# Weights' words joined by two VectorE operations out of PSUM, squares of two quads on TensorE, smaller first MLP groups, a new order

## The chip, the core and the metric

The kernel runs on one core of a Trainium2 chip. Its engines are TensorE (PE in the profile), VectorE (DVE), ScalarE (ACT), GpSimd (POOL) and SyncE (SP), which here issues nearly all DMAs from one queue, in order. The metric is the device time of one launch in microseconds; lower is better.

## What is computed

```python
scores = scale * np.matmul(q, k.transpose(0, 1, 3, 2))          # 4 batches, 8 heads, 576 x 576, head size 64
thresh = np.max(scores, axis=-1, keepdims=True) - tau
scores = np.where(scores >= thresh, scores, -1000000000.0)
attn = softmax(scores); x = np.matmul(attn, v)                  # heads side by side: x is (4, 576, 512)
...
xn = (x - mu) / np.sqrt(var + 1e-06) * g_ln
x = x + np.maximum(xn @ w_ch1, 0.0) @ w_ch2                     # 512 -> 2048 -> 512
...
theta = x @ w_theta
y = w_tok_r @ (x * cos(theta)) + w_tok_i @ (x * sin(theta))     # mixes the 576 tokens
u = x + y; out = u + np.maximum(u @ w_ch, 0.0)
```

Everything is f32 outside. Inside, a matmul of f32 accuracy is three fp16 matmuls: each operand is scaled by a power of two and split into a high and a low fp16 part.

## The kernel before

**Three kinds of work.** (1) Attention: 36 units of 128 query rows for each of the 4 batches, 144 in all; two heads are done together as a "couple" of two units (one unit for the half tile at a batch's end). A unit is a QK product on PE (tile `S`), the row minimum on VectorE (`top`), a mask and an exp on ScalarE, a high fp16 part (`hi16`) and a low one (`lo16`) on whichever of VectorE, GpSimd, ScalarE the plan picks, a transposing DMA of the result (`PT`), and the product with V on PE (`pv`). (2) The MLP on the finished tokens: nine tiles of 128 tokens for batches 0 and 1 ("the first half"), nine for batches 2 and 3. Tiles go in groups of three; for each group a layer norm, a transpose on PE (`ptr`, split into `xt`), and 16 chunks, each a first product (`p`, 12 matmuls whose moving operand is the group's 384 tokens) and a second one (`ch`, 3 matmuls of 512 columns per tile). (3) The token mixing (`th`, `y`, `o`) from about 640 us on.

**Weights.** w1 and w2 come as 32 pieces of 128 x 512 in four "quads" of eight; `th`, `tok` and `cw` are 20 more. Their two 32-bit halves arrive as pairs of integers (`raw`) and are joined into f32 words on the chip (class `Piece`): `s1` scales the high half (GpSimd or ScalarE), `s1b` the low half (ScalarE), `s2b` and `s2c` shift and put in the sign (VectorE), `s3` adds the low half (GpSimd). `sq` squares the words on ScalarE to find the scale (`pow2` sums over partitions and rounds to a power of two), and `split` makes the two fp16 parts. A quad of `HOME` (0 and 1) has its raw words loaded into the 16 weight buffers themselves; the others go through a ring of three raw buffers.

**The order is planned by the program itself.** `Plan.run` is a list scheduler: each operation has costs for the engines that may do it, due-time offsets by kind (`OFF`), extra costs of an engine (`PEN`) and buffers that it takes and gives back (`Slot`, `Res`). The instructions are written out on each engine in the order that this plan finds; on the chip each engine runs them strictly in that order and waits by semaphores. Where the plan sees PE idle for over 200 ns before `turn`, `keep` writes warming matmuls (`warm`) into the gap. Four PSUM banks (`rM`) serve `p`, `ch`, `pv`, `ptr` and the small sums; two more pairs serve `S`.

Of the kernel before, what the change touches and what calls it, by code (L numbers as in the profile page):

```python
# [21 lines left out]
DM = 512  # L22
KB = 4
# [37 lines left out]
HPA = 0.0  # L61
# [6 lines left out]
MX = 1  # L68
# [140 lines left out]
def tile_kernel(  # L209
# [39 lines left out]
    def vc(n, x=1.04):  # L249
        return 157.0 + x * n  # L250
# [54 lines left out]
    def n_tile(slot, name):  # L305
        return lp.tile([128, 512], F32, tag=str(slot), name=name)
# [57 lines left out]

    warm = Slot(rM)
# [20 lines left out]
    class Piece:  # L386


        def __init__(self, src, shape, ss, col, name, start, kind, home=False, by=None):
# [12 lines left out]

            def s1(e):
                st["a"] = n_tile(sa, f"a_{name}")[:, 0:n]
                if e is G:
                    G.tensor_scalar(out=st["a"], in0=st["rw"][:, :, 1].bitcast(F32), scalar1=DOWN, scalar2=0.0,  # L406
                                    op0=ALU.mult, op1=ALU.add)
                else:
                    A.activation(out=st["a"], in_=st["rw"][:, :, 1].bitcast(F32), func=AF.Copy, scale=DOWN)

            def s1b(e):
                rw = st["rw"]
                A.activation(out=rw[:, :, 0], in_=rw[:, :, 0].bitcast(U32), func=AF.Copy, scale=2.0 ** -29)
# [22 lines left out]
            o = op(s2b, [o], V=vc(n, .95), **kw)
            o = op(s2c, [o], (), [sa], V=vc(n, 1.45), **kw)
            self.done = last_s3[0] = op(s3, [o, ob, last_s3[0]], () if home else (self.sf,), () if home else (sl,), G=gadd(n), **kw)
            self.sq = op(sq, [self.done] + ([] if by is None else [k_load]), A=ac(n) + 130.0, **kw)

        def split(self, hi, lo, sc, deps, acq=()):
# [17 lines left out]
            return op(s5, [o], (), [self.sf], V=vc(n, 1.4), G=2000, **kw)  # L459

    def pow2(nm, ss, n, top, deps, dst, kind):
# [24 lines left out]
        o = op(add_up, [o], (), (ms,), V=170, **kw)  # L486
# [16 lines left out]
    class Quad:  # L503


        def __init__(self, q, prev):
# [312 lines left out]
    def unit(st, us, o_qk, pen0, kw, cp):  # L819
# [136 lines left out]
    def ln_group(p, gi, base):  # L956
# [85 lines left out]
        for r0, r1 in zip(ROUNDS, ROUNDS[1:]):  # L1042
            qd = quads[r0 // 4]
            for t in range(nt):
                ms = Slot(rM)
                o = None
                for i in range(r0, r1):
# [10 lines left out]
                    o = op(mm, [o or hs[r1 - 1][3], hs[i][2], chunks[i].c2], (ms,) if i == r0 else (), rel, T=3 * mm_(512),  # L1058
# [88 lines left out]
    def split_weight(name, src_list, start, sc, kind="cvt"):  # L1147
# [523 lines left out]
```

## Time and profile before

| | |
|---|---|
| median of 3 runs | 890.38 us (890.22 to 890.48) |
| profiled execution, its own time | 890.8 us |
| its span, first to last instruction | 889.0 us |
| mean granted TensorE clock | 0.984 of full speed |
| busy: PE, DVE, ACT, POOL | 836.2, 670.4, 575.8, 503.4 us |
| PE's part in it that is `warm` filling | 70.1 us |

Busy time is the union of an engine's instructions. PE looks busy for 94% of the span, but 70 us of this are matmuls whose result nobody reads. The shares change much between the stages, so the stages are read apart.

### The profile page before, as it was taken

How to read it: one execution, taken by the hardware profiler on the slowest of the kernel's cores; microseconds unless marked ns; L12 is line 12 of the kernel's file. 1: busy time of each engine (PE TensorE's matmuls, PEld its weight loads, DVE VectorE, ACT ScalarE, POOL GpSimd, SP SyncE). 2: the span in 40 equal slices, each digit the busy share in tenths (PEclk: the TensorE clock that was granted, in tenths of full speed). 3: DMA queues.
4: the chain of work that ended last, by engine and by line, in shares of the span. 5: the costliest groups of instructions: out<-in, count | busy, mean ns of one | idle time of the engine just before them, and what ended most of it. 6: DMA issues, size and time to landing. Idle time of an engine off the chain costs nothing.

```text
span 889.0 us, 19045 instructions
## 1 busy us (share of the span) xinstructions
PE 836.2 (94%) x7368; PEld 563.5 (63%) x7368; DVE 670.4 (75%) x1250; ACT 575.8 (65%) x1075; POOL 503.4 (57%) x554
## 2 busy tenths in 40 slices
PE   9687777999999999999999999999999799989997
PEld 8575566656666666675666556555556477666776
DVE  5999999979898874795278725666688974699943
ACT  6787887777898875895388724555567542465512
POOL 5999999887657851692067403343437570064910
PEclk9899999999999999999999999999999899999999
DMA  8955888846799744891566428234213011020011
GB/s 278 255 127 138 161 189 166 210 93 93 136 187 201 140 94 94 162 173 31 127 115 109 81 57 196 64 119 150 75 36 107 25 36 54 1 77 1 1 55 54
DMA packets 209211, 99.36 MB, mean 112 GB/s; under 512 B 173280, under 2 KB 193760, under 8 KB 209120
## 3 DMA queue, kind: packets, MB, share of 16 engines
q1 hardware_dynamic: 208832, 98.14, 49.1%
q8 instruction: 58, 0.95, 0.5%
q14 instruction: 33, 0.27, 0.1%
q10 hardware_dynamic: 288, 0.00, 0.0%
HBM read 46.21 MB, written 9.44 MB: 63 GB/s over the span
## 4 chain that ended last, share of the span: by engine, by line
PE 68%; DVE 15%; POOL 10%; issue 5%; DMA 1%; ACT 1%; DVEq 0%; POOLq 0%; SPq 0%
PE ch L598 20%; PE p L575 20%; PE S L770 6%; PE y L1491 6%; PE pv L792 6%; PE o L1549 3%; PE th L1315 2%; POOL ringP L241 2%; POOL ringP L238 2%; DVE z L1380 1%; DVE raw_w L422 1%; POOL a_w L406 1%; POOL f_w L426 1%; DVE ringE L830 1%; PE warm L371 1%
## 5 line engine op out<-in xcount | busy, mean ns | idle before, releaser
L598 PE MATMUL ch<-w,h 128*128 128x512 f16 x864 | 199.8, 379 | 0.3 <-DVE x L1063 0.3
L575 PE MATMUL p<-xt,w 128*128 128x384 f16 x1152 | 198.2, 326 | 0.0
L241 POOL TENSOR_TENSOR ringP<-ringE,ringP 128x512 f16<-128x512 f32 (+2 forms) x146 | 144.2, 1001 | 54.2 <-DVE h L584 29.1
L575 PEld LDWEIGHTS <-w 128*128 128x128 f16 x1152 | 110.0, 98 | 73.2 <-issue 2.8
L598 PEld LDWEIGHTS <-h 128*128 128x128 f16 x864 | 81.5, 98 | 90.0 <-issue 3.5
L830 DVE TENSOR_SCALAR_CACHE_REDUCE ringE<-S 128x576 f32<-128x576 f32 x144 | 104.6, 748 | 15.7 <-PE S L770 13.2
L770 PE MATMUL S<-khi,q 64*128 64x288 f32 (+1 forms) x576 | 85.2, 328 | 28.6 <-DVE ringE L830 25.2
L846 ACT ACTIVATE ringE<-ringE,thr 128x576 f32<-128x576 f32 x144 | 105.6, 767 | 7.5 <-POOL thr L838 5.5
L876 ACT ACTIVATE ringE<-ringE,ntaup 128x576 f32<-128x576 f32 x144 | 104.2, 764 | 0.1
L1491 PE MATMUL y<-tok,z 128*128 128x288 f16 x768 | 99.6, 289 | 0.0
L1063 DVE SCALAR_TENSOR_TENSOR x<-ch,inv,x 128x512 f32<-128x512 f32 x72 | 53.7, 747 | 58.0 <-PE ch L598 57.8
L238 POOL TENSOR_SCALAR ringP<-ringE 128x576 f16<-128x576 f32 x93 | 68.6, 744 | 49.3 <-ACT ringE L876 48.2
L581 ACT ACTIVATE h<-p 128x384 f16<-128x384 f32 x96 | 46.8, 488 | 71.0 <-PE p L575 70.4
L1491 PEld LDWEIGHTS <-z 128*128 128x128 f16 x768 | 76.1, 99 | 21.0
L584 DVE SCALAR_TENSOR_TENSOR h<-p,h 128x384 f16<-128x384 f32 x96 | 52.5, 550 | 45.7 <-ACT h L581 45.0
L792 PEld LDWEIGHTS <-PT 128*128 128x128 f16 (+1 forms) x2240 | 77.1, 101 | 14.6 <-issue 5.6
L770 PEld LDWEIGHTS S<-khi,q 64*128 64x128 f32 (+1 forms) x576 | 55.6, 191 | 48.5 <-DVE ringE L830 31.1
L792 PE MATMUL pv<-va,PT 128*128 128x65 f16 (+1 forms) x2240 | 81.2, 194 | 1.4 <-DMA PT<-ringP 0.9
L241 DVE TENSOR_TENSOR ringP<-ringE,ringP 128x512 f16<-128x512 f32 (+1 forms) x78 | 70.6, 918 | 3.9 <-POOL ringP L238 3.0
L379 PE MATMUL warm<-one 128*128 128x256 bf16 x538 | 70.1, 286 | 0.0
L379 PEld LDWEIGHTS <-one 128*128 128x128 bf16 x538 | 53.4, 104 | 10.6 <-issue 2.8
L1549 PE MATMUL o<-x1T,cw 128*128 128x288 f16 x384 | 48.2, 286 | 2.5 <-POOL x1T L241 2.5
(246 smaller groups left out, 1398.4 us busy)
## 6 DMA issues: line engine op xcount, KB each, us to landing
raw_w<-in_w SPq DMA_DIRECT2D x32, 512.0 KB, 4.7
raw_tok<-in_wtok SPq DMA_DIRECT2D x12, 432.0 KB, 3.3
qraw<-in_qT SPq DMA_DIRECT2D x20, 256.0 KB, 3.4
vraw<-in_v SPq DMA_DIRECT2D x16, 320.0 KB, 4.7
kraw<-in_kT SPq DMA_DIRECT2D x16, 288.0 KB, 4.0
xfin<-x SPq DMA_DIRECT2D x18, 256.0 KB, 2.0
xl<-xfin SPq DMA_DIRECT2D x18, 256.0 KB, 3.3
out<-uo SPq DMA_DIRECT2D x16, 288.0 KB, 2.1
```

Source lines behind the costliest of these rows:

```text
L238: G.tensor_scalar(out=out, in0=in_, scalar1=1.0, scalar2=0.0, op0=ALU.mult, op1=ALU.add)
L241: e.tensor_tensor(out=out, in0=a, in1=b, op=ALU.subtract)
L379: T.matmul(w[:, 0:256], lhsT=one16[:, 0:128], rhs=one16, start=True, stop=True)
L575: T.matmul(st["ps"][:, :n], lhsT=ch.w1(a, c), rhs=xt()[:, c, bb, :n], start=(kk == 0), stop=(kk == 11))
L598: T.matmul(ps, lhsT=h[:, a, t * 128:(t + 1) * 128], rhs=ch.w2(bb), start=(first and (a, bb) == M2[0]), stop=(stop and (a, bb) == M2[2]))
L770: T.matmul(w["S"][:, n, 0:288], lhsT=qd.q["t"][r, a, hp], rhs=d.k[bb][r, n * 288:(n + 1) * 288], start=(k == 0), stop=(k == 2))
L792: T.matmul(out[:, j * 65:j * 65 + n], lhsT=l, rhs=r[:, j * 65:j * 65 + n], start=(k == 0), stop=(k == len(seq) - 1))
L830: V.tensor_scalar(out=st["e"].rearrange("p (a k) -> p a k", a=2), in0=st["S"][:, :, 0:288], scalar1=-1.0, scalar2=None, op0=ALU.mult, op1= ...
L846: A.activation(out=st["e"], in_=st["e"], func=AF.Prelu, bias=cp["thr"][:, j:j + 1], scale=-1.0, alpha=STEEP)
L876: A.activation(out=e_of(ws), in_=e_of(ws), func=AF.Exp, bias=ntaup, scale=1.0)
L1491: T.matmul(st["ps"][n][:, 0:288], lhsT=a, rhs=w[:, n * 288:(n + 1) * 288], start=(k == 0 and q == 0), stop=(k == 8 and q == 2))
L1549: T.matmul(st["ps"][n][:, 0:288], lhsT=w[:, cs], rhs=d["t"][a][:, kk, n * 288:(n + 1) * 288], start=(kk == 0 and q == 0), stop=(kk == 3 an ...
```

## The change

The joining of words loses `s2b`, `s2c` and GpSimd's add. ScalarE alone now scales the high half, and writes it to one of the four `rM` banks of PSUM (tile `a`); VectorE then takes the sign from it into the low half (`s2`) and shifts it by three bits over the low half (`s3`), both times reading `a` out of PSUM. For quads 0 and 1 the squares come from PE: each 128 x 128 block of a piece, its words' upper halves read as bf16, is multiplied by itself into one bank (`gram`), and VectorE reads the largest entry. No quad is at home any more: all pieces load into the ring of three raw buffers. The first half's MLP groups hold two, two, two and three tiles in place of three times three. The exp of a couple's two units is one instruction (`MX = 2`). The constants that set the order are new.

```diff
-CVQ = (8000.0, 30000.0, 30000.0, 30000.0)
-CVD = 2300.0
-HOME = (0, 1)
-GROUPS = (((0, 3), (3, 3), (6, 3)), ((0, 3), (3, 3), (6, 3)))
+CVQ = (8000, 36900, 69900, 8000)
+CVD = 3600.0
+HOME = ()
+SQ = 'TTAA'
+SQP = 'A'
+GROUPS = (((0, 2), (2, 2), (4, 2), (6, 3)), ((0, 3), (3, 3), (6, 3)))
...
-HPA = 0.0
+HPA = 1500.0
...
-MX = 1
+MX = 2
...
-            sa = Slot(rN)
+            sa = Slot(rM)
...
             def s1(e):
-                st["a"] = n_tile(sa, f"a_{name}")[:, 0:n]
-                if e is G:
-                    G.tensor_scalar(out=st["a"], in0=st["rw"][:, :, 1].bitcast(F32), scalar1=DOWN, scalar2=0.0,
-                                    op0=ALU.mult, op1=ALU.add)
-                else:
-                    A.activation(out=st["a"], in_=st["rw"][:, :, 1].bitcast(F32), func=AF.Copy, scale=DOWN)
+                st["a"] = m_tile(sa, [128, 512], f"a_{name}")[:, 0:n]
+                A.activation(out=st["a"], in_=st["rw"][:, :, 1].bitcast(F32), func=AF.Copy, scale=DOWN)
...
-            def s2b(e):
-                a = st["a"].bitcast(U32)
-                V.tensor_scalar(out=st["rw"][:, :, 1].bitcast(U32), in0=a, scalar1=3, scalar2=0x7FFFFFF8,
-                                op0=ALU.logical_shift_left, op1=ALU.bitwise_and)
-
-            def s2c(e):
-                a, y = st["a"].bitcast(U32), st["rw"][:, :, 1].bitcast(U32)
-                V.scalar_tensor_tensor(out=y, in0=a, scalar=0x80000000, in1=y, op0=ALU.bitwise_and, op1=ALU.bitwise_or)
+            def s2(e):
+                low = st["rw"][:, :, 0].bitcast(U32)
+                V.scalar_tensor_tensor(out=low, in0=st["a"].bitcast(U32), scalar=0x80000000, in1=low, op0=ALU.bitwise_and,
+                                       op1=ALU.bitwise_or)
 
             def s3(e):
...
-                G.tensor_tensor(out=st["w"].bitcast(I32), in0=st["rw"][:, :, 1], in1=st["rw"][:, :, 0], op=ALU.add)
+                V.scalar_tensor_tensor(out=st["w"].bitcast(U32), in0=st["a"].bitcast(U32), scalar=3,
+                                       in1=st["rw"][:, :, 0].bitcast(U32), op0=ALU.logical_shift_left, op1=ALU.bitwise_or)
...
+                    for k in range(0, n, 128):
+                        T.matmul(stats.ps[:, 0:128], lhsT=w[:, k:k + 128], rhs=w[:, k:k + 128], start=(col == 0 and k == 0),
+                                 stop=(col == 3 and k + 128 == n))
```

The order shows where this moves the work. First place: VectorE, where the first MLP group's operand `xt_0_0` is finished; `ringE,bt_b_t_h` is the row minimum of the couple of batch b, tile t, heads h. Before:

```order
L830 TENSOR_SCALAR ringE_83,bt_1_4_0_0_2309<-S_1_4_0_0_2280 128x576
L241 TENSOR_TENSOR xt_0_0_2265<-ptr_0_0_1_2273,xt_0_0_2265 128x4x128
L241 TENSOR_TENSOR xt_0_0_2265<-ptr_0_0_2_2299,xt_0_0_2265 128x4x128
L241 TENSOR_TENSOR ringP_84<-ringE_83,ringP_84 128x512
L417 TENSOR_SCALAR raw_w1_12_3_2185<-a_w1_12_3_2332 128x512
```

And with the change:

```order
L920 TENSOR_SCALAR ringE_83,bt_0_3_1_0_1510<-S_0_3_1_1_1449 128x576
L243 TENSOR_TENSOR xt_0_0_1528<-ptr_0_0_0_1512,xt_0_0_1528 128x4x128
L563 TENSOR_SCALAR sc_1_114<-t2_w2_1_119 128x1
L567 TENSOR_SCALAR sc_1_114<-sc_1_114 128x1
L446 SCALAR_TENSOR_TENSOR raw_w1_8_2_1415<-a_w1_8_2_1561,raw_w1_8_2_1415 128x512
L243 TENSOR_TENSOR xt_0_0_1528<-ptr_0_0_1_1521,xt_0_0_1528 128x4x128
```

The operand was finished behind the minimum of couple 1_4_0 (the 21st), with the pieces of quad 3 (`w1_12`) already under way; now it is finished behind couple 0_3_1 (the 14th), with quad 2 (`w1_8`) at its third piece. Second place: VectorE in quad 1, the joining of words. Before:

```order
L417 TENSOR_SCALAR raw_w1_4_2_644<-a_w1_4_2_762 128x512
L417 TENSOR_SCALAR raw_w1_4_3_710<-a_w1_4_3_786 128x512
L684 SCALAR_TENSOR_TENSOR va_0_3_548<-vraw_0_3_313,vscale0_91,va_0_3_548 128x10x64
L422 SCALAR_TENSOR_TENSOR raw_w1_4_2_644<-a_w1_4_2_762,raw_w1_4_2_644 128x512
L830 TENSOR_SCALAR ringE_83,bt_0_1_1_0_935<-S_0_1_1_0_873 128x576
L830 TENSOR_SCALAR ringE_83,bt_0_1_1_0_935<-S_0_1_1_1_874 128x576
L422 SCALAR_TENSOR_TENSOR raw_w1_4_3_710<-a_w1_4_3_786,raw_w1_4_3_710 128x512
```

And with the change:

```order
L446 SCALAR_TENSOR_TENSOR raw_w1_4_2_810<-a_w1_4_2_915,raw_w1_4_2_810 128x512
L446 SCALAR_TENSOR_TENSOR raw_w1_4_3_895<-a_w1_4_3_966,raw_w1_4_3_895 128x512
L451 SCALAR_TENSOR_TENSOR f_w1_4_2_996<-a_w1_4_2_915,raw_w1_4_2_810 128x512
L920 TENSOR_SCALAR ringE_83,bt_0_2_0_0_1002<-S_0_2_0_0_977 128x576
L451 SCALAR_TENSOR_TENSOR f_w1_4_3_1018<-a_w1_4_3_966,raw_w1_4_3_895 128x512
```

There are still two VectorE operations for a piece, but `a` now lies in PSUM and the second one gives the finished word `f`, so GpSimd's add behind it is gone. Third place: SP's queue, the same quad. Before:

```order
L898 DMA_TRANSPOSE PT_0_0_1_1_551<-ringP_84 128x9x128
L401 DMA raw_w1_4_0_596<-in_w1 128x1024
L401 DMA raw_w1_4_1_632<-in_w1 128x1024
L401 DMA raw_w1_4_2_644<-in_w1 128x1024
L401 DMA raw_w1_4_3_710<-in_w1 128x1024
L401 DMA raw_w2_4_0_756<-in_w2 128x1024
L401 DMA raw_w2_4_1_768<-in_w2 128x1024
L898 DMA_TRANSPOSE PT_0_0_2_0_782<-ringP_84 128x9x128
```

And with the change:

```order
L434 DMA raw_w1_4_0_704<-in_w1 128x1024
L434 DMA raw_w1_4_1_718<-in_w1 128x1024
L990 DMA_TRANSPOSE PT_0_0_3_0_759<-ringP_84 128x9x128
L990 DMA_TRANSPOSE PT_0_0_3_1_773<-ringP_84 128x9x128
L434 DMA raw_w1_4_2_810<-in_w1 128x1024
L990 DMA_TRANSPOSE PT_0_1_0_0_820<-ringP_84 128x9x128
L990 DMA_TRANSPOSE PT_0_1_0_1_868<-ringP_84 128x9x128
L434 DMA raw_w1_4_3_895<-in_w1 128x1024
```

The loads of quad 1 stood in a row, each into a buffer of its own; now they stand one or two at a time between the transposes, each waiting for one of three raw buffers.

## Rows read from the trace of the kernel before

**Rows 1.** Busy time by stage; columns: length, PE, PEld, DVE, ACT, POOL, clock, DMA.

```profile
0.00:157.00 157.00, 122.14 (x1287) 101.91 (x1288) 142.59 (x254) 124.34 (x231) 142.13 (x159) 0.93 0.78 188
157.00:296.00 139.00, 138.16 (x1440) 88.50 (x1437) 121.81 (x252) 113.95 (x221) 100.36 (x122) 1.00 0.79 154
296.00:640.00 344.00, 343.81 (x3003) 210.42 (x3001) 219.15 (x457) 219.31 (x427) 155.53 (x196) 1.00 0.52 112
640.00:889.00 249.00, 232.13 (x1645) 162.65 (x1643) 186.84 (x290) 118.22 (x199) 105.37 (x80) 0.98 0.12 40
```

**Rows 2.** The same view, the warming matmuls of L379 alone (PE, PEld).

```profile
0.00:157.00 157.00, 70.11 (x538) 53.40 (x538) 0.93 0.78 188
```

**Rows 3.** Tile p, first 200 us: shortest, median, longest; first and last start.

```profile
L575 PE MATMUL p<-xt,w x96: 322/326/337, 156.9 to 188.1; 128*128 128x384 f16 x96
```

**Rows 4.** Who waited for whom, 0 to 157: total us, times, longest.

```profile
PE S L770 <- DVE ringE L830: 25.0, 22, 3.6
```

**Rows 5.** Groups by shape, 0 to 157: busy us, mean ns, idle before.

```profile
L422 DVE SCALAR_TENSOR_TENSOR raw_w<-a_w,raw_w 128x512 uint32<-128x512 uint32 x27 | 32.3, 1201 | 0.0
L830 DVE TENSOR_SCALAR_CACHE_REDUCE ringE<-S 128x576 f32<-128x576 f32 x37 | 26.8, 746 | 2.5 <-PE S L770 2.1 <-POOL ringP L241 0.4
L241 POOL TENSOR_TENSOR ringP<-ringE,ringP 128x512 f16<-128x512 f32 x18 | 26.0, 1446 | 0.0
L238 POOL TENSOR_SCALAR ringP<-ringE 128x576 f16<-128x576 f32 x30 | 25.2, 849 | 0.7 <-ACT ringE L876 0.7
L426 POOL TENSOR_TENSOR raw_w<-raw_w 128x512 int32<-128x512 int32 x16 | 20.1, 1258 | 0.7 <-DVE raw_w L422 0.7
L417 DVE TENSOR_SCALAR raw_w<-a_w 128x512 uint32<-128x512 uint32 x27 | 19.4, 730 | 1.2 <-POOL a_w L406 1.2
L241 DVE TENSOR_TENSOR ringP<-ringE,ringP 128x512 f16<-128x512 f32 x16 | 18.5, 1163 | 1.3 <-POOL ringP L238 1.3
L452 DVE SCALAR_TENSOR_TENSOR w<-raw_w,sc,w 128x512 f16<-128x512 f32 x13 | 16.1, 1279 | 0.0
L406 POOL TENSOR_SCALAR a_w<-raw_w 128x512 f32<-128x512 f32 x17 | 14.4, 845 | 0.6 <-DVE raw_w L422 0.6
L426 POOL TENSOR_TENSOR f_w<-raw_w 128x512 int32<-128x512 int32 x10 | 12.8, 1280 | 0.0
L409 ACT ACTIVATE a_w<-raw_w 128x512 f32<-128x512 f32 x11 | 7.3, 665 | 2.5 <-DVE raw_w L422 2.5
```

**Rows 6.** Groups by shape, 157 to 296.

```profile
L241 POOL TENSOR_TENSOR ringP<-ringE,ringP 128x512 f16<-128x512 f32 x20 | 23.8, 1192 | 0.8 <-ACT ringP L234 0.4
L238 POOL TENSOR_SCALAR ringP<-ringE 128x576 f16<-128x576 f32 x33 | 23.1, 707 | 21.0 <-ACT ringE L876 21.0
L1063 DVE SCALAR_TENSOR_TENSOR x<-ch,inv,x 128x512 f32<-128x512 f32 x16 | 11.8, 744 | 3.6 <-PE ch L598 3.4
```

**Rows 7.** PE in order of time at 296 us.

```profile
296.42 0.53 PE L770 MATMUL S<-khi,q 64*128 64x288 f32 x4
```

**Rows 8.** Busy time by stage of L770 (S), then L575 (p), L598 (ch), L792 (pv).

```profile
0.00:156.90 156.90, 31.83 (x228) 23.39 (x228) 0.93 0.78 188
156.90:296.40 139.50, 23.47 (x252) 18.18 (x252) 1.00 0.79 154
...
156.90:296.40 139.50, 50.31 (x288) 26.94 (x288) 1.00 0.79 154
...
156.90:296.40 139.50, 46.73 (x198) 18.32 (x198) 1.00 0.79 154
...
156.90:296.40 139.50, 24.96 (x679) 23.02 (x675) 1.00 0.79 154
```

**Rows 9.** The page's group of matmuls with 288 columns.

```profile
L1491 PE MATMUL y<-tok,z 128*128 128x288 f16 x768 | 99.6, 289 | 0.0
```

**Rows 10.** SP's own waits, 0 to 157.

```profile
SPq L401 <- POOL f_w L426: 7.4, 6, 2.3
```

More of the change, by code (lines that the diff above doesn't have):

```diff
@@ L363, in tile_kernel, with g_square, g_turn, g_top @@
     k_pool = op(c_pool, [k_ones], G=1200, kind="prep")
+    gg = const.tile([128, KB], F32, name="gg")
+    gmax = const.tile([128, 1], F32, name="gmax")
+    gtop = const.tile([128, 1], F32, name="gtop")
+    gt, sg = {}, Slot(rM)
+    def g_square(e):
+        V.tensor_tensor(out=gg, in0=gsb, in1=gsb, op=ALU.mult)
+    def g_turn(e):
+        gt["ps"] = psM.tile([128, 512], F32, tag=str(sg), name="gtop_ps")
+        T.matmul(gt["ps"][0:KB, 0:128], lhsT=gg, rhs=ident, start=True, stop=True)
+    def g_top(e):
+        V.tensor_scalar(out=gt["ps"][0:KB, 0:128], in0=gt["ps"][0:KB, 0:128], scalar1=1.0, scalar2=None, op0=ALU.mult, op1=ALU.max,
+                        accum_out=gmax[0:KB])
+    def g_sum(e):
+        T.matmul(gt["ps"][:, 256:257], lhsT=ones[0:KB], rhs=gmax[0:KB], start=True, stop=True)
+    def g_keep(e):
+        V.tensor_copy(out=gtop, in_=gt["ps"][:, 256:257])
+    o = op(g_square, [k_load], V=120, kind="prep")
+    o = op(g_turn, [o, k_pool], (sg,), T=230, key=-1e6, kind="prep")
+    o = op(g_top, [o], V=300, kind="prep")
+    o = op(g_sum, [o, k_ones], T=60, key=-1e6, kind="prep")
+    k_top = op(g_keep, [o], (), (sg,), V=160, kind="prep")
     warm = Slot(rM)
@@ L432, in __init__ @@
             kw = dict(kind=kind)
             self.load = op(s0, start, (sl,), Q=1800, **kw)
-            o = op(s1, [self.load], [sa], A=ac(n) + 40.0, G=gs(n), **kw)
             ob = op(s1b, [self.load], A=ac(n), **kw)
[L436 to L439, printed above, removed]
+            o = op(s1, [self.load], [sa], A=ac(n) + 40.0, **kw)
@@ L441, in split @@
+            o = op(s2, [o, ob], V=vc(n, 1.15), **kw)
+            self.done = last_s3[0] = op(s3, [o, last_s3[0]], () if home else (self.sf,), (sa,) if home else (sa, sl), V=vc(n, 1.15), **kw)
+            if how == "T":
+                self.sq = op(sq, [self.done] + stats.deps, () if col else (stats.sl,), T=n / 128.0 * mm_(128), key=-9e5, **kw)
+                stats.deps = [self.sq]
+            else:
+                self.sq = op(sq, [self.done], **cost(how, n), **kw)
         def split(self, hi, lo, sc, deps, acq=()):
@@ L458, in split, with measure, __init__, __call__ @@
             o = self.hi_op = op(s4, [self.done, self.sq] + deps, acq, A=ac(n) + 93.0, V=vc(n, .95), **kw)
[L459 to L461 removed]
+            return op(s5, [o], (), [self.sf], V=vc(n, 1.4), G=gr(n), **kw)
+    def measure(out, in_, acc):
+        A.activation(out=out, in_=in_, func=AF.Square, accum_out=acc)
+    class Stats:
+        def __init__(self, nm):
+            self.nm, self.t = nm, None
+            self.sl, self.ps, self.deps = Slot(rM), None, []
+        def __call__(self):
+            if self.t is None:
+                self.t = sm.tile([128, 4, 6], F32, tag="st4", bufs=4, name="st_" + self.nm)
+            return self.t
+    def cost(how, n):
+        return {"A": ac(n) + 130.0} if how == "A" else {"V": vc(n)}
+    def squares_of(how, ss, n, stats_, deps, kind, by=None):
+        if how == "A" and by is None:
+            return deps
+        def go(e):
+            if how == "T":
+                V.tensor_scalar(out=stats_.ps[:, 0:128], in0=stats_.ps[:, 0:128], scalar1=1.0, scalar2=None, op0=ALU.mult, op1=ALU.max,
+                                accum_out=ss[:, 0:1])
+                return
+            if how == "V":
+                stats = stats_()
+                V.tensor_tensor(out=stats[:, :, 0:5:4], in0=stats[:, :, 1:5:3], in1=stats[:, :, 1:5:3], op=ALU.mult)
+                V.scalar_tensor_tensor(out=stats[:, :, 2:6:3], in0=stats[:, :, 0:5:4], scalar=n / 2.0,
+                                       in1=stats[:, :, 2:6:3], op0=ALU.mult, op1=ALU.add)
+                V.tensor_tensor(out=ss, in0=stats[:, :, 2], in1=stats[:, :, 5], op=ALU.add)
+            if by is not None:
+                V.tensor_tensor(out=ss, in0=ss, in1=by, op=ALU.mult)
+                V.tensor_tensor(out=ss, in0=ss, in1=by, op=ALU.mult)
+        if how == "T":
+            return [op(go, deps, (), (stats_.sl,), V=360, kind=kind)]
+        return [op(go, deps, V=(420 if how == "V" else 0) + (0 if by is None else 280), kind=kind)]
+    def pow2(nm, ss, n, top, deps, dst, kind, by=None):
         st, ms = {}, Slot(rM)
@@ L536, in parts @@
                 return ends
-            rm1 = const.tile([128, KB], F32, name=f"rm1_{q}")
-            p1 = pieces("w1", [w1[c * 128:(c + 1) * 128, fc * 256:fc * 256 + 1024] for c in range(KB)], rm1, True)
-            o1 = pow2(f"w1_{q}", rm1, KB, W1_TOP, [pc.sq for pc in p1], sc[:, 0:1], kd)
+            gram = SQ[q] == "T"
+            nr = 1 if gram else KB
+            rm1 = const.tile([128, nr], F32, name=f"rm1_{q}")
+            p1, st1 = pieces("w1", [w1[c * 128:(c + 1) * 128, fc * 256:fc * 256 + 1024] for c in range(KB)], rm1)
+            o1 = squares_of(SQ[q], rm1, DM, st1, [k_load] + [pc.sq for pc in p1], kd, None if gram else gsb)
+            o1 = pow2(f"w1_{q}", rm1, nr, W1_TOP, o1, sc[:, 0:1], kd, gtop if gram else None)
             def gscale(e):
@@ L891, in go @@
             def go(e):
-                sub(e, p_of(ws)[:, :, 576:640], e_of(ws)[:, :, 512:576], p_of(ws)[:, :, 512:576])
+                crossed = len(ws) == 2 and (ws[0]["es"].i < ws[1]["es"].i) != (ws[0]["s16"].i < ws[1]["s16"].i)
+                for w_ in ([[w] for w in ws] if crossed else [ws]):
+                    sub(e, p_of(w_)[:, :, 576:640], e_of(w_)[:, :, 512:576], p_of(w_)[:, :, 512:576])
             return go
```

55 lines of the change are left out of this document (35 added, 20 removed).

## The prediction

> **What bounds the kernel now.** I read the busy time by stage first [rows 1]. From 157 to 640 us PE is busy for 481.97 of 483 us: whatever else happens there is free. Before 157 us PE shows 122 us of work, but 70.1 us of it are warming matmuls [rows 2], so with 35 us idle it does only some 52 us of real work in 157. VectorE and GpSimd are busy for 142 us each in that stretch, ScalarE for 124, and the DMA engines for 78%. The list of waits says the same from PE's side: QK products wait 25.0 us, in 22 pieces, for VectorE's row minimum [rows 4]. The border is sharp: the first MLP matmul starts at 156.9 us [rows 3], and from there PE has a stock of MLP work to fall back on.
>
> So I cut the run into three. **A** lasts to the first MLP matmul (156.9 us). **B** lasts to the QK product of couple 2_1_0, found in the trace by counting S matmuls against the order (480 of them stand before it); it starts at 296.4 us [rows 7]. **C** is the rest, 592.6 us to the span's end. A is bound by VectorE and GpSimd, B by PE, C by PE but for some 17 us between 640 and 889 [rows 1]. The time is the sum of the three.
>
> **A: when MLP work can start.** The order puts the first MLP matmul behind 15 couples' QK products instead of 22, with 19 pieces of weights joined by VectorE instead of 27. What each engine has ahead of that point is counted from the order and priced by the rows of A.
>
> VectorE, from 142.6 us [rows 1]: the joins fall from 27 x (1.201 + 0.730) = 51.7 us [rows 5] to 19 + 18 operations. The new form, one input in PSUM and one in SBUF, is not in this trace. The nearest from below is the MLP's update `x<-ch,inv,x`, two f32 inputs of 512, one of them in PSUM: 0.744 [rows 6]. From above it is the old join with everything in SBUF, 1.201. The first is the nearer by operands, so 37 x 0.744 = 27.5, a saving of 24.2 us (7.3 by the upper bound). Row minima fall from 37 to 28 (0.746 plus some 0.08 for reading the result: 7.4 us). Low parts on VectorE fall from 16 to 4 of the 512-wide form (1.163 each) and by five small ones, about 19 us; fp16 parts of weights from 17 to 10, about 8; ten high parts come, about 5. Smaller things (K and Q parts, scalings) take off another 8. That leaves about 81 us (98 by the upper bound).
>
> GpSimd, from 142.1: its 26 adds (20.1 + 12.8) and 17 scalings (14.4) go, 47.3 us. High parts fall from 30 to 14 (0.849 each, 13.6), low parts rise from 18 to 20 (2.9), Q's and K's parts rise by about 8 in place of other small work that falls by 4. About 87 remain (80 if low and high parts take B's 1.192 and 0.707 [rows 6]). ScalarE keeps about 82 of 124 us: fewer couples, no squares, exps of two units together. Transposes and loads fall by about 28%, so DMA keeps some 88 of 122.
>
> The longest engine's idle time was 157 - 142.6 = 14.4 us, mostly the start. GpSimd's 87 plus that, and 3 because four resources are now nearly equal, gives **105 us**; bounds 95 (80 + 14.4) and 120 (VectorE at 98, plus 14.4, plus 8 of mutual waiting).
>
> PE's own additions in A, the 64 `gram` products of 128 columns and their sums, cost at most 64 x 0.13 = 8 us, the warming row's price for twice the columns (70.11 / 538) [rows 2]. They lie in PE's idle time, which is still over half of A; without that cover they would cost those 8 us.
>
> [...] The rows of A show where the old joins lost their time: `s2c` takes 1.201 us on average, the PSUM form 0.744 [rows 5, 6], and VectorE's row minimum, out of PSUM, 0.746 in a stage where GpSimd is busy 91% of the time. [...] By the rows the old pair cost 1.93 us in A and the new one 1.49, so there the sum stands.
>
> **B: the same way further with more work in it.** In A fewer couples were done, so B holds 25 couples' worth of QK (300 S matmuls against 252), 456 first products of 256 tokens against 288 of 384, 216 second ones against 198, 812 `pv` against 672. A 256-token product is not in the trace: 384 columns cost 50.31 / 288 = 0.175 us [rows 8], 288 columns 99.6 / 768 = 0.130 [rows 9]; the line through both gives 0.115, and 0.130 is the upper bound. So 52.4 + 27.9 + 51.0 + 30.1 = 161.4 us where the same sum for before is 145.5 and PE's time was 139.5: PE needs **155 us**. GpSimd has 46 high parts (32.5 us by [rows 6]), 41 wide low ones (48.9), 11 weight parts of two operations each (some 24, between the 0.845 and 1.280 of such forms in A [rows 5]) and some 59 of small low parts, K, Q, V, thresholds and scalings: about 164. The same count gives VectorE about 153, ScalarE about 154. Before, GpSimd had 39 us to spare in B; high parts that ScalarE did now sit on it. I take GpSimd's 164 plus 5% for waits: **172 us**; 156 if everything hides behind PE, 189 if GpSimd meets VectorE as in A (15% more).
>
> **C.** PE has 18 second products fewer (4.2 us) and 96 of the wide first products fewer for 120 narrow ones (3.0): 592.6 less 7 is **586 us**. The 20 pieces of `th`, `tok`, `cw` are joined while PE works on the MLP; they are hidden by that, and PE's real waits after 640 us I leave as they are. [...]
>
> **Sum.** 105 + 172 + 586 = 863. The profiled execution lies 1.8 us above its span (890.8 - 889.0) and the median 0.4 below it, so 864.4: I say **864 us**, 26 less than before.
>
> **Rivals.**
>
> 1. *The vector engines stay the bound in B.* For it: GpSimd, VectorE and ScalarE are all within 10 us of each other and none has the reserve that B has now. Against it: contention in B was mild (1.192 against 1.446) and three of VectorE's largest forms read PSUM. 864 + 17 = **881 us**.
> 2. *Everything hides.* A ends at 98 and B is PE's 155: **840 us**. For it: no filling is left in B's order. Against it: in A now the fullest engine reaches only 91%.
> 3. *PE runs slow in A.* Warming matmuls fall from 538 to 185. In A the granted clock is already 0.93 on average, and an S matmul costs 0.140 us there against 0.093 in B [rows 8]. [...] At half of B's speed A's 180 S matmuls would take 0.186, 8 us more than at A's present rate, with `pv` behind them up to 16: **880 us**. Against it: PE waits for VectorE in A anyway.
> 4. *SP's queue.* All loads now wait for one of three raw buffers, and transposes stand behind them in one queue. Before, SP waited 7.4 us in six waits for the raw ring in A [rows 10], for ten pieces. If each of the 32 pieces holds the transposes back by 0.8 us on the chain, the gain is gone: **890 us**, no change.
> 5. *PSUM banks (slower).* Each piece holds one of the four banks that PE's MLP chains use, from ScalarE's copy (0.665 [rows 5]) to VectorE's second operation, 2.2 us at least. 29 pieces come after A, where PE has no slack. If PE stands for half of that, 1.1 us each, it loses 32 us: **896 us**. It decides the sign from 0.9 us per piece. Against it: VectorE takes the second operation soon behind the first in the order.
>
> **Chances.** My forecast 0.45, everything hides 0.17, vector engines in B 0.20, slow PE 0.06, SP's queue 0.05, banks 0.07. From 848 to 886 lie the forecast, the nearer half of "hides" and nearly all of the 0.26 above it: 8 in 10. A measurement of this kernel can tell about 0.2% from no change: faster 0.88, within it 0.05, slower 0.07.
>
> **What would show it.** The first MLP matmul near 105 us (A); the QK of 2_1_0 near 277 (A + B); from there 586 to the end. The two join operations near 0.744 us each with little spread, also while GpSimd works. PE idle in B under 20 us: well above that, GpSimd busy throughout says rival 1, PE's matmuls ended by waits for a PSUM reader of `a` says rival 5. S matmuls in A above 0.140 say rival 3, PE waiting for PT says rival 4. The forecast is wrong if A does not end before 125 us, or if B takes 190.

## The result and the profile after

The changed kernel takes **854.66 us** (median of 4 runs, 851.43 to 856.97) against 890.43 for the kernel before: a ratio of 0.9588, 95% interval 0.9545 to 0.963. The forecast was 864, range 848 to 886. The profiled execution took 856.97 with a span of 855.2. Runs of the changed kernel lie up to 5.5 us apart, so differences of 2 or 3 us between kernels like it mean nothing here.

Stretch A, to the first MLP matmul, ends at 100.1 us; B, to the QK product of couple 2_1_0, at 269.8. In busy time by stage of the kernel after (columns as in [rows 1]; the last two rows together are C):

```profile
0.00:100.10 100.10, 74.82 (x806) 62.17 (x807) 79.84 (x179) 80.51 (x135) 78.62 (x104) 0.86 0.97 215
100.10:269.80 169.70, 160.29 (x1827) 118.84 (x1823) 152.91 (x334) 139.21 (x268) 151.01 (x190) 1.00 0.87 176
269.80:640.00 370.20, 367.29 (x3157) 226.63 (x3157) 258.99 (x519) 224.42 (x422) 158.26 (x193) 1.00 0.50 106
640.00:855.20 215.20, 203.42 (x1496) 147.18 (x1494) 151.94 (x221) 100.67 (x169) 113.27 (x86) 0.98 0.12 41
```

| stretch | before | forecast | after |
|---|---|---|---|
| A | 156.9 | 105 | 100.1 |
| B | 139.5 | 172 | 169.7 |
| C | 592.6 | 586 | 585.4 |

A is 57 us shorter, B 30 longer, C 7 shorter. In A, VectorE, ScalarE and GpSimd are now within 2 us of each other. Groups by shape in A of the kernel after (columns as in [rows 5]):

```profile
L243 POOL TENSOR_TENSOR ringP<-ringE,ringP 128x512 f16<-128x512 f32 x21 | 26.7, 1276 | 0.3
L860 PE MATMUL S<-khi,q 64*128 64x288 f32 x120 | 20.9, 370 | 9.9 <-DVE ringE L920 9.7 <-DVE q L821 0.2
L446 DVE SCALAR_TENSOR_TENSOR raw_w<-a_w,raw_w 128x512 uint32<-128x512 uint32 x19 | 12.8, 679 | 0.0
L451 DVE SCALAR_TENSOR_TENSOR f_w<-a_w,raw_w 128x512 uint32<-128x512 uint32 x18 | 12.3, 682 | 0.1
L240 POOL TENSOR_SCALAR ringP<-ringE 128x576 f16<-128x576 f32 x16 | 11.8, 741 | 6.1 <-ACT ringE L966 6.1
L463 PE MATMUL gram_w<-f_w 128*128 128x128 bf16 x64 | 7.3, 244 | 13.1 <-DVE f_w L451 9.1 <-DVE sc L567 2.5 <-DVE sc L563 1.6
```

The 37 join operations are there as counted, at 0.68 us (25.1 in all, where the pairs of [rows 5] came to 51.7), and GpSimd's additions are gone. The same view in B:

```profile
L665 PE MATMUL p<-xt,w 128*128 128x256 f16 x456 | 55.6, 273 | 2.6 <-DVE f_w L451 1.9 <-ACT x L236 0.4 <-DVE vscale L763 0.2
L243 POOL TENSOR_TENSOR ringP<-ringE,ringP 128x512 f16<-128x512 f32 x39 | 48.0, 1232 | 0.6 <-DVE ringP L238 0.4
L240 POOL TENSOR_SCALAR ringP<-ringE 128x576 f16<-128x576 f32 x43 | 34.4, 806 | 8.2 <-ACT ringE L966 5.2 <-DMA PT<-ringP 2.8
```

Who waited for whom (total, times, longest), in A:

```profile
PE S L860 <- DVE ringE L920: 9.7, 6, 3.8
PE gram_w L463 <- DVE f_w L451: 9.1, 8, 3.4
...
SPq L434 <- DVE f_w L451: 16.2, 10, 3.5
```

and in B:

```profile
PE p L665 <- DVE f_w L451: 1.9, 2, 1.4
...
PE pv L882 <- DMA PT<-ringP: 0.3, 1, 0.3
```

PE's waits for row minima in A have fallen from the 25.0 us of [rows 4] to 9.7. SP waits longer for the raw ring than in [rows 10] (16.2 against 7.4), but PE waited only 0.3 us for a transpose in B. The row `p L665 <- DVE f_w L451` is read as PE waiting for the bank that `a` held, since `f_w` is the last operation that reads `a`: 1.9 us.

### The profile page after: what moved, and what is told of

Read it like the earlier page. It is cut to its first block, busy times and chain, and to the rows that moved or that the text cites. A ratio compares the mean times of both kernels' runs of the same rounds, so it can differ in the third digit from the quotient of the medians.

```text
span 855.2 us, 18703 instructions
## 1 busy us (share of the span) xinstructions
PE 805.8 (94%) x7275; PEld 554.8 (65%) x7275; DVE 643.7 (75%) x1250; ACT 544.8 (64%) x992; POOL 501.2 (59%) x571
## 4 chain that ended last, share of the span: by engine, by line
PE 68%; DVE 12%; POOL 9%; issue 5%; ACT 4%; DMA 1%; POOLq 0%; DVEq 0%
PE p L665 19%; PE ch L688 19%; PE y L1584 9%; PE S L860 6%; PE pv L882 6%; PE th L1408 5%; POOL ringP L243 2%; DVE ringE L920 2%; PE o L1642 2%; POOL w L243 1%; POOL ringP L240 1%; PE warm L404 1%; POOL f_w L493 1%; DVE r L1429 1%; ACT ringE L936 1%
## 5 line engine op out<-in xcount | busy, mean ns | idle before, releaser
L665 PE MATMUL p<-xt,w 128*128 128x384 f16 (+1 forms) x1344 | 200.6, 303 | 3.0 <-DVE f_w L451 1.9
L665 PEld LDWEIGHTS <-w 128*128 128x128 f16 x1344 | 128.4, 99 | 62.8 <-issue 6.9
L243 POOL TENSOR_TENSOR ringP<-ringE,ringP 128x512 f16<-128x512 f32 (+2 forms) x177 | 163.2, 940 | 5.1 <-DVE ringP L238 3.1
L240 POOL TENSOR_SCALAR ringP<-ringE 128x576 f16<-128x576 f32 x114 | 86.0, 762 | 59.1 <-ACT ringE L966 31.6
L936 ACT ACTIVATE ringE<-ringE,thr 128x576 f32<-128x576 f32 x144 | 106.0, 768 | 11.8 <-POOL thr L928 9.5
L860 PE MATMUL S<-khi,q 64*128 64x288 f32 (+1 forms) x576 | 86.1, 331 | 11.8 <-DVE ringE L920 10.9
L671 ACT ACTIVATE h<-p 128x384 f16<-128x384 f32 (+1 forms) x112 | 49.0, 440 | 72.5 <-PE p L665 72.1
L966 ACT ACTIVATE ringE<-ringE,ntaup 128x1152 f32<-128x1152 f32 (+1 forms) x80 | 92.2, 1154 | 0.9
L674 DVE SCALAR_TENSOR_TENSOR h<-p,h 128x384 f16<-128x384 f32 (+1 forms) x112 | 54.8, 493 | 46.1 <-ACT h L671 45.7
L243 DVE TENSOR_TENSOR ringP<-ringE,ringP 128x512 f16<-128x512 f32 (+2 forms) x64 | 53.4, 847 | 6.2 <-POOL ringP L240 6.0
L1408 PE MATMUL th<-th,x1T 128*128 128x512 f16 x192 | 45.4, 393 | 2.9 <-DVE x1T L1382 2.9
L1611 POOL TENSOR_TENSOR u<-u,x1T 128x576 f32<-128x576 f32 x14 | 20.8, 1484 | 44.3 <-DVE u L1606 44.3
```

What stands on the lines that cost most here:

```text
L240: G.tensor_scalar(out=out, in0=in_, scalar1=1.0, scalar2=0.0, op0=ALU.mult, op1=ALU.add)
L665: T.matmul(st["ps"][:, :n], lhsT=ch.w1(a, c), rhs=xt()[:, c, bb, :n], start=(kk == 0), stop=(kk == 11))
L860: T.matmul(w["S"][:, n, 0:288], lhsT=qd.q["t"][r, a, hp], rhs=d.k[bb][r, n * 288:(n + 1) * 288], start=(k == 0), stop=(k == 2))
L936: A.activation(out=st["e"], in_=st["e"], func=AF.Prelu, bias=cp["thr"][:, j:j + 1], scale=-1.0, alpha=STEEP)
L966: A.activation(out=e_of(ws), in_=e_of(ws), func=AF.Exp, bias=ntaup, scale=1.0)
L1408: T.matmul(st["ps"], lhsT=src(a, c), rhs=w[:, c * 512:(c + 1) * 512], start=(kk == 0), stop=(kk == 11))
```

## The experiments

Twelve more kernels ran. The table gives each one's median, ratio to the kernel before with its interval, and the three stretches of its profiled execution, cut as above.

| kernel | median | ratio | A | B | C |
|---|---|---|---|---|---|
| after | 854.66 | 0.9588 (0.9545 to 0.963) | 100.1 | 169.7 | 585.4 |
| pe_dose | 858.66 | 0.9639 (0.9625 to 0.9653) | 96.6 | 174.4 | 585.5 |
| pool_dose | 858.64 | 0.9638 (0.9622 to 0.9654) | 98.7 | 175.3 | 584.4 |
| dma_dose | 856.94 | 0.9621 (0.9592 to 0.9649) | 99.8 | 169.5 | 583.6 |
| a_sbuf | 873.16 | 0.9805 (0.9788 to 0.9821) | 106.5 | 179.0 | 584.0 |
| u_groups | 865.86 | 0.9713 (0.9688 to 0.9739) | 122.9 | 144.5 | 595.2 |
| b_groups | 881.92 | 0.9898 (0.9877 to 0.992) | 124.3 | 172.6 | 585.4 |
| u_numbers | 880.42 | 0.9886 (0.9857 to 0.9915) | 98.5 | 174.9 | 604.0 |
| u_squares | 854.57 | 0.9591 (0.9571 to 0.9611) | 95.5 | 173.4 | 583.5 |
| b_grnum | 889.7 | 0.9992 (0.9982 to 1.0003) | 117.1 | 178.3 | 592.8 |
| u_mxhpa | 861.26 | 0.967 (0.9655 to 0.9684) | 94.5 | 170.3 | 593.9 |
| u_off | 855.12 | 0.9603 (0.9587 to 0.9619) | 96.5 | 171.7 | 584.0 |
| no_fill | 853.64 | 0.958 (0.9565 to 0.9596) | 98.5 | 167.6 | 584.0 |

The stretches hold differing amounts of the MLP where the order differs; in kernels of the changed order they can be set side by side. The first QK product starts between 9.2 and 11.8 us in these profiles (11.1 in the changed kernel's own), so an A that differs by 2 us is no difference.

### Which engine sets B: doses of work in the same order

The program's planner was given the same costs, so each engine's order is that of the changed kernel.

**pe_dose.** 108 more products on PE in B.

```diff
+                    for _ in range(3 if kk == 0 and n == 256 and dose[0] <= 36 else 0):
+                        T.matmul(st["ps"][:, :n], lhsT=ch.w1(a, c), rhs=xt()[:, c, bb, :n], start=True, stop=True)
```

> The changed kernel in the same order, with more work on PE: 36 of the chains of MLP first products with 256 tokens get their first product three times more, 108 products in all. At the 0.122 us of such a product in the changed kernel (55.5 us for 456) that is 13.1 us of PE, all of it between the first MLP matmul and the QK of couple 2_1_0 (stretch B, 169.7 us, PE busy 160.3, GpSimd 151.0). If PE sets B: 11 to 13 us longer, 865 to 868. If GpSimd sets B, as the prediction had it: the 9.4 us in which PE is idle take most of it, 3 to 5 us longer, 857 to 860.

**pool_dose.** 15 more high parts on GpSimd.

```diff
+                    if 16 < dose[0] <= 60 and dose[0] % 3 == 0:
+                        copy(e, p_of(ws)[:, :, 0:576], e_of(ws))
```

> The changed kernel in the same order, with more work on GpSimd: 15 of its rounded high parts in stretch B are computed twice, 15 x 0.806 = 12.1 us. If GpSimd sets B, as the prediction had it: 10 to 12 us longer, 864 to 867. If PE sets B: GpSimd's 18.7 idle us of B take it, 0 to 4 us longer, 854 to 859.

**dma_dose.** Eight more transfers in A.

```diff
+                if dose[0] <= 16 and dose[0] % 2 == 0:
+                    Q.dma_start(drp.tile([128, 2 * n], I32, tag=f"more{dose[0]}", name=f"more{dose[0]}"), src)
```

> The changed kernel in the same order, with more transfers: behind every second of the first 16 loads of weights' pieces SP issues a second transfer of the same 512 KB, to a place in DRAM that nobody reads: 8 transfers, 4.2 MB on top of the 21.5 MB of stretch A (to the first MLP matmul, 100.1 us, DMA share 0.97). At A's mean rate (21.5 MB in 0.97 x 100.1 us) that is 19 us of all queues' time. If the DMA engines set A: 15 to 19 us longer, 870 to 874. If the vector engines do, as the prediction had it, and transfers have room: 0 to 4 us longer, 854 to 859.

B in the busy time by stage of pe_dose:

```profile
96.60:271.00 174.40, 169.79 (x1934) 128.43 (x1930) 152.14 (x334) 139.91 (x270) 149.97 (x190) 1.00 0.88 175
```

of pool_dose:

```profile
98.70:274.00 175.30, 162.18 (x1827) 119.02 (x1822) 155.84 (x334) 140.03 (x269) 160.25 (x204) 1.00 0.87 172
```

and A of dma_dose:

```profile
0.00:99.80 99.80, 76.86 (x805) 62.75 (x806) 80.22 (x179) 80.16 (x134) 78.20 (x104) 0.83 1.06 252
```

PE's dose raised its busy time by 9.5 us (13.1 were forecast), B by 4.7 and the median by 4.0. GpSimd's raised its busy time by 9.2, B by 5.6 and the median by 4.0. Each median lies in the range that its expectation gave for the *other* engine as the one that sets B (857 to 860, and 854 to 859); that can't be so for both. How much of a dose comes through is known only roughly. A ended earlier in these two, and the three kernels of this order without a dose in B (the changed one, dma_dose and no_fill) have medians from 853.6 to 856.9, so 2 to 5 us of the 9 came through. That is enough to say that neither PE (97% busy under its dose) nor GpSimd sets B alone. VectorE, busy for 152.9 us of B and so longer than GpSimd, got no dose: whether it sets B is open. The chain that ended last passes in B of the changed kernel through PE for some 45% of the time, VectorE for 21, GpSimd for 12 and ScalarE for 11, which also speaks for a mixture.

A took the additional transfers for nothing: the share rose from 0.97 to 1.06, and A and the whole stayed within the runs' spread. The DMA engines do not set A. The transfers themselves did take longer, though; the transposes' median time from issue to landing in A, in the changed kernel and then in dma_dose, is the last number:

```profile
PT<-ringP SPq DMA_TRANSPOSE x24, 4.8
...
PT<-ringP SPq DMA_TRANSPOSE x24, 5.8
```

### What the PSUM operand is worth

**a_sbuf.** The scaled word stays in SBUF.

```diff
-                st["a"] = m_tile(sa, [128, 512], f"a_{name}")[:, 0:n]
+                st["a"] = st["rw"][:, :, 1].bitcast(F32)
```

> The changed kernel in the same order, but ScalarE writes the scaled word a back into the raw buffer in SBUF instead of into a PSUM bank, and VectorE's two joins read it there; the bank stays reserved, so that nothing else moves. By the theory that the PSUM operand is what made the joins cheap beside GpSimd: 0.68 us becomes some 1.2 us in stretch A, as the old form had it, 37 x 0.5 = 19 us more on VectorE there, A 8 to 15 us longer, the whole 860 to 872. By the rival that the cheaper form comes from the operations alone: the joins stay within 0.65 to 0.78 us, the whole 852 to 858.

Groups by shape in A of a_sbuf:

```profile
L243 POOL TENSOR_TENSOR ringP<-ringE,ringP 128x512 f16<-128x512 f32 x21 | 29.0, 1386 | 0.3
...
L451 DVE SCALAR_TENSOR_TENSOR f_w<-raw_w 128x512 uint32<-128x512 uint32 x19 | 19.9, 1048 | 1.2 <-POOL w L243 1.1
L446 DVE SCALAR_TENSOR_TENSOR raw_w<-raw_w 128x512 uint32<-128x512 uint32 x19 | 19.0, 1002 | 0.1
L240 POOL TENSOR_SCALAR ringP<-ringE 128x576 f16<-128x576 f32 x16 | 14.4, 908 | 1.8 <-ACT ringE L966 1.8
```

The same two operations cost 1.00 and 1.05 us instead of 0.68, and GpSimd's own became dearer too (1.386 against 1.276, 0.908 against 0.741): GpSimd is busy 93.1 us in this A instead of 78.6. The median rose by 18.5 us, to 1 us above the expected range. The profiled span rose by 14.3, of which 6.4 are in A (8 to 15 were expected) and 9.3 in B; C did not grow. There the pieces of `th` (four) and `tok` (twelve) tell why. In C of a_sbuf, of the changed kernel and of the kernel before, each in the view by shape:

```profile
L446 DVE SCALAR_TENSOR_TENSOR raw_tok<-raw_tok 128x432 uint32<-128x432 uint32 x12 | 8.3, 689 | 0.9 <-ACT raw_tok L438 0.9
...
L446 DVE SCALAR_TENSOR_TENSOR raw_th<-raw_th 128x512 uint32<-128x512 uint32 x4 | 2.8, 693 | 1.1 <-ACT raw_th L438 1.1
```

```profile
L446 DVE SCALAR_TENSOR_TENSOR raw_tok<-a_tok,raw_tok 128x432 uint32<-128x432 uint32 x12 | 7.2, 602 | 1.2 <-ACT a_tok L438 1.2
...
L446 DVE SCALAR_TENSOR_TENSOR raw_th<-a_th,raw_th 128x512 uint32<-128x512 uint32 x4 | 2.8, 688 | 1.1 <-ACT a_th L438 1.1
```

```profile
L422 DVE SCALAR_TENSOR_TENSOR raw_th<-a_th,raw_th 128x512 uint32<-128x512 uint32 x4 | 2.7, 684 | 0.0
...
L417 DVE TENSOR_SCALAR raw_th<-a_th 128x512 uint32<-128x512 uint32 x4 | 2.1, 533 | 0.0
```

Where GpSimd is busy less than half of the time (158 of 370 us), SBUF and PSUM cost the same for `th`, 0.69. For `tok` SBUF's mean is 0.69 against 0.60, but its median is 0.61: a few operations took up to 1.13. So what the PSUM operand saves is time on both engines where both work at once: from SBUF the first join took 1.00 us beside a GpSimd busy for 93.1 of 106.5 us and 0.69 beside a quiet one, from PSUM 0.68 and 0.69, and GpSimd's own two operations took 1.386 and 0.908 against 1.276 and 0.741. By what path the two engines hinder each other, no run shows.

Nor does a run test apart whether an operand in PSUM makes an operation slower beside a quiet GpSimd. The old shift alone, with one input from SBUF, has a mean of 0.533 in C, and three of its four operations on `th` took 0.42 (shortest, median and longest):

```profile
L417 DVE TENSOR_SCALAR raw_th<-a_th x4: 418/419/877, 560.7 to 575.4; 128x512 uint32<-128x512 uint32 x4
```

No join of 512 elements that reads PSUM took less than 0.63; but the joins from SBUF, with their two inputs, stay at 0.69 in C as well, so the second input may be the reason as much as PSUM. By the means the old pair cost 1.22 in C against the new pair's 1.37, and in A 1.93 against 1.36.

### What each part is worth

In these the program plans a new order, so more moves than the edit. The `u_` kernels are the changed one with a part undone, the `b_` kernels the one before with a part added.

**u_groups** and **b_groups.** Groups of three again; groups of two alone.

```diff
-GROUPS = (((0, 2), (2, 2), (4, 2), (6, 3)), ((0, 3), (3, 3), (6, 3)))
+GROUPS = (((0, 3), (3, 3), (6, 3)), ((0, 3), (3, 3), (6, 3)))
```

> The changed kernel with the first half's MLP groups of three tiles again; joins, squares and order numbers stay as changed. The first MLP matmul then stands behind 222 S matmuls in the order instead of 180, so three and a half couples more. If the order that groups of two allow is the main part of the gain: A grows by 3.5 couples at some 6 us each (100 us for 15, start included), to about 120, and little of it comes back in B; 868 to 878. If the joins are the main part: A grows by less than 8 us, and wider products give part of it back in B, 854 to 862.

> The kernel before with one part of the change alone: the first half's MLP groups of two, two, two and three tiles. Its order puts the first MLP matmul behind 180 S matmuls instead of 228; the joins stay the old ones, with GpSimd's additions. If the order is the main part of the gain: 866 to 876. If it needs the cheap joins, because the vector engines bind A and B with the old ones: 878 to 890.

**u_numbers**, **u_mxhpa** and **u_off.** All of the order's numbers back; two of them; the others.

```diff
-HPA = 1500.0
-MX = 2
+HPA = 0.0
+MX = 1
...
-CVQ = (8000, 36900, 69900, 8000)
-CVD = 3600.0
-PEN = {"V": 1200.0, "A": 650.0, "G": 500.0}
+CVQ = (8000.0, 30000.0, 30000.0, 30000.0)
+CVD = 2300.0
+PEN = {"V": 1000.0, "A": 500.0, "G": 500.0}
```

with `CQ` and `OFF` of the kernel before. u_mxhpa has the first two lines alone, u_off all but these.

> The changed kernel with the numbers that set the order put back (due times of the weights' loads, offsets by kind, penalties, one exp for each unit instead of one for two); groups, joins and squares stay as changed. 180 S matmuls still stand before the first MLP matmul. If the groups and joins carry the gain: 855 to 863. If the numbers carry a large part: over 868.

> The changed kernel with two of the numbers put back: one exp for each unit instead of one for two, and no penalty on ScalarE for the rounded high parts, which puts more than 50 of them on ScalarE where the changed order has none. If this is what made the old numbers cost 26 us, by ScalarE's work and by GpSimd's waits for it: 870 to 880. If the loads' due times and the offsets by kind made it: 854 to 862.

> The changed kernel with the other numbers put back: due times of the weights' loads, offsets by kind and the penalties for leaving an engine; exps of two units in one and ScalarE's penalty for high parts stay as changed. If these made the old numbers cost 26 us: 868 to 880. If ScalarE's load made it: 854 to 862.

**u_squares.**

```diff
-SQ = 'TTAA'
+SQ = 'AAAA'
```

> The changed kernel with the squares of the first two quads on ScalarE again, 16 of 0.622 us (the row of squares in B), instead of 64 products of 128 columns on PE. By the prediction's step, ScalarE is not the longest engine of A by far (80.5 us busy against GpSimd's 78.6 and VectorE's 79.8 in 100.1), but level with them: 10 us more on ScalarE makes A 4 to 10 us longer, 858 to 866. If it hides: 852 to 857.

**b_grnum.** The kernel before with the new `GROUPS` and all the new numbers. The changed kernel's line for couples whose units lie crossed in the two rings is not in it, so the last 64 low parts of such couples are taken from the other unit, in one operation where the changed kernel has two.

> The kernel before with two parts of the change, the groups of two and the numbers that set the order (exps of two units in one among them); the joins stay the old ones with GpSimd's additions, the squares on ScalarE. 168 S matmuls stand before the first MLP matmul. If the new joins matter with these numbers: some 19 additions of 1.26 us and the scalings come back to GpSimd in A, and VectorE's pairs at 1.9 instead of 1.36 us; A 15 to 25 us longer than the changed kernel's 100, the whole 868 to 882. If groups and numbers suffice, as the 1.5 us between the old joins with groups (881.9) and the new joins with groups and squares (880.4), both with the old numbers, would have it: 853 to 860.

*Groups*: 11 us when taken out, 8.6 when alone. u_groups ends A at 122.9, as the first theory had it, but its B is 25 us shorter and its C 10 longer than the changed kernel's: work moved from one to the other. Its 866 lies between the two readings.

*Squares*: nothing (854.57 against 854.66). ScalarE's additional 3 us in A (83.8 busy against 80.5) hid.

*Joins and numbers* don't add up. With groups of two throughout:

| | old joins | new joins |
|---|---|---|
| old numbers | 881.92 (b_groups) | 880.42 (u_numbers) |
| new numbers | 889.7 (b_grnum) | 854.66 (after) |

(The right column has PE's squares, which cost nothing, and the raw ring for all quads too; the ring was not tried apart.) The new joins save 1.5 us with the old numbers, which is within the runs' spread, and 35 with the new ones; the new numbers lose 8 with the old joins and save 26 with the new. The 1.5 us hide more than they show: from b_groups to u_numbers A falls from 124.3 to 98.5, and B and C together grow by 21. The 889.7 of b_grnum lies above both ranges of its expectation (868 to 882, 853 to 860), though its A is 17 us longer, as the first had it. In A of b_grnum the joins are as dear as they were (0.94 each) and GpSimd, busy for 104.4 of the 117.1 us, has its additions (groups by shape):

```profile
L417 DVE TENSOR_SCALAR raw_w<-a_w 128x512 uint32<-128x512 uint32 x21 | 19.7, 944 | 0.3 <-POOL a_w L406 0.3
L422 DVE SCALAR_TENSOR_TENSOR raw_w<-a_w,raw_w 128x512 uint32<-128x512 uint32 x21 | 19.6, 938 | 0.1
L426 POOL TENSOR_TENSOR raw_w<-raw_w 128x512 int32<-128x512 int32 x16 | 19.3, 1206 | 1.3 <-DVE raw_w L422 0.6 <-DVE sc L481 0.6
```

u_numbers reaches its first MLP matmul at 98.5, no later than the changed kernel, and loses in B, where it has done 384 first products instead of 456. Its busy time in three stretches of B:

```profile
140.00:160.00 20.00, 11.60 (x119) 8.90 (x117) 19.68 (x41) 19.23 (x37) 17.17 (x25) 0.80 0.86 172
180.00:200.00 20.00, 13.22 (x139) 8.63 (x138) 19.19 (x40) 17.37 (x35) 18.41 (x21) 0.99 1.00 175
200.00:220.00 20.00, 17.23 (x160) 12.61 (x161) 16.96 (x38) 16.29 (x31) 16.48 (x20) 0.76 0.71 126
```

and the same in the changed kernel:

```profile
140.00:160.00 20.00, 18.79 (x206) 14.33 (x206) 18.37 (x45) 17.26 (x34) 17.95 (x24) 1.00 0.96 213
180.00:200.00 20.00, 19.04 (x292) 14.85 (x292) 17.27 (x44) 16.74 (x37) 16.23 (x22) 1.00 0.84 142
200.00:220.00 20.00, 20.00 (x225) 15.14 (x224) 18.61 (x42) 14.11 (x25) 19.24 (x23) 1.00 0.59 91
```

PE, in the first column, stands for 18 of these 60 us in u_numbers and for 2 in the changed kernel. From 140 to 160 us it did 12 first products there against 39, and its waits ended on VectorE:

```profile
PE pvs L753 <- DVE vsc L756: 3.4, 1, 3.4
PE S L860 <- DVE ringE L920: 3.2, 3, 1.9
PE p L665 <- DVE xt L243: 1.6, 1, 1.6
```

So PE waited at products of the attention, with few MLP products between them in its order. The third quad's w2 has its scale at 175 us there against 145, the fourth's w1 at 200 against 184, so the order probably had no weights to put MLP products on; that is argued from the times, not shown. In that B GpSimd waits for ScalarE's high parts, which the changed order does not put there:

```profile
POOL ringP L243 <- ACT ringP L236: 15.4, 7, 8.7
```

Undone apart, exps and high parts cost 6.6 us, the other numbers 0.5; undone together, 26. Each run came out as its expectation said for the case that the other half is the cause, which can't be so for both: it takes the two together. Why is not settled.

### PE's clock in A

**no_fill.** The filling matmuls of the gaps left out, in the same order.

```diff
-BUSY = 0.7
+BUSY = 0.0
```

> The changed kernel in the same order without the 185 filling matmuls of stretch A (26.4 us of PE), which write a bank that nobody reads. If PE's clock in A matters, as the prediction's rival of the slow clock had it: the granted clock of A falls under its 0.86, S matmuls cost over 0.14 us against 0.122, and A is 5 to 15 us longer, the whole 860 to 870. If PE waits for the vector engines in A anyway: the whole 852 to 858.

A of no_fill, all engines and then the S matmuls alone:

```profile
0.00:98.50 98.50, 66.39 (x620) 54.81 (x621) 81.54 (x179) 80.72 (x135) 78.57 (x104) 0.65 0.94 218
...
0.00:98.50 98.50, 30.69 (x180) 22.84 (x180) 0.65 0.94 218
```

The granted clock fell from 0.86 to 0.65 and an S matmul rose from 0.122 us (22.03 / 180) to 0.171, above the 0.140 of the rival, and A did not grow. PE's speed in A has no price, because PE waits for VectorE's row minima either way, 9.7 us in the changed kernel and in A of no_fill:

```profile
PE S L860 <- DVE ringE L920: 11.8, 14, 2.5
```

The kernel is as fast without its 185 filling matmuls (853.64).

## Why the prediction was right, point by point

**A, 105 forecast, 100.1 measured.** The cut at the first MLP matmul and the counts from the order held. Of the terms, VectorE (81) measured 79.8, ScalarE (82) 80.5, the joins (27.5) 25.1. "GpSimd's 87", the term that made GpSimd the longest engine, was too large by 8. Some 5 of these are its low and high parts, 1.276 and 0.741 us instead of the 1.446 and 0.849 carried over from [rows 5], since the joins no longer meet them; a_sbuf, which brings the meeting back, has 1.386 and 0.908. The idle time beside the longest engine, 17 in the sum, was 19.6. DMA's share was 0.97 where 88 of 105 us had been said; dma_dose shows that it does not matter.

**gram.** 7.33 us on PE within its idle 25, hidden as said. What the text did not ask is whether the squares' leaving ScalarE gains anything; u_squares says no.

**B, 172 forecast, 169.7 measured, right by luck: the step behind it was wrong.** "GpSimd's 164 plus 5% for waits" took GpSimd as what sets B. GpSimd took 151: its wide parts came to 82.4 against 81.4 forecast, but the "some 59" of small operations came to 45 (151.0 less 82.4 and the weight parts' 23.2). PE took 160.3, not 155 (a product of 256 tokens 0.122 instead of 0.115, S matmuls 0.108, 32.70 / 302, instead of the 0.093 of [rows 8]). By the doses neither sets B alone, and VectorE was not tried. GpSimd 13 too high and a bound that does not hold cancelled each other, and the stretch came out 2 us off.

**C, 586 forecast, 585.4 measured.** The matmuls that had moved ahead of it, and nothing else; the 20 late pieces hid, and would have from SBUF too (a_sbuf: 584.0). Beside a quiet GpSimd the new pair costs 0.15 us more per piece of `th` than the old one by the means (1.37 against 1.22).

**Rivals.** Vector engines the bound in B: a part of GpSimd's dose came through and a part of PE's too, so at most a part of the truth. Everything hides: A came near its 98, B did not. Slow PE in A: an S matmul took 0.122 us, under the 0.140 of its condition; the condition held in no_fill (0.171), and its price was nil. Half of B's speed, 0.186 in its sum, was the author's supposition; neither kernel shows it. SP's queue: SP waits for the ring, PE for no transpose that counts. Banks: 1.9 us in B, far from 32.

**Parts.** The sum priced the built order, joins and numbers together, which is probably why it came out: a sum of edits, each measured alone beside groups of two, would have given the joins 1.5 us and the numbers a loss.

## What to carry to other kernels

Where a program plans its own order, count what stands ahead of a milestone in the order as built and price it by rows of the same stage; parts measured one by one say little, since here one was worth nothing and another a loss, and together they were most of the gain. To learn which engine sets a stretch, give each a known dose in the same order, large against the spread of the runs: here only a part of either dose came through, so neither engine was the bound alone. An operand in PSUM paid here where VectorE and GpSimd worked at the same time, on both engines (a join 0.68 us against 1.00, GpSimd's subtraction 1.276 against 1.386); beside a quiet GpSimd it saved nothing, or 0.09 us.

## What the runs showed of the hardware that was not expected

- The DMA share went to 1.06 in A, with eight 512 KB transfers more, and A ended no later, though the transposes' median time to landing rose from 4.8 to 5.8 us: a share near 1 in the profile is no proof of a bound.
- GpSimd's subtraction of 512 elements has a mean of 1.276 us beside joins from PSUM and 1.386 beside joins from SBUF, and its high part 0.741 and 0.908: the choice of VectorE's operand is seen on the other engine.
- With the granted clock at 0.65 over all of A, A was as long as at 0.86 (98.5 us against 100.1), though an S matmul took 0.171 us instead of 0.122.
